# Six convolution units for eight in a spectral-mixing kernel, with transposes, late rows and one bank's products moved

## The chip, the cores and the metric

The kernel runs on one core of a Trainium2 chip. A core has five engines with queues of their own: TensorE (PE, with its weight loads as PEld), VectorE (DVE), ScalarE (ACT), GpSimd (POOL) and SyncE (SP). Here POOL issues all loads, which cast float32 in HBM to bfloat16 in the on-chip memory, and SP issues the stores. The metric is the device time of one execution in microseconds (us). The kernel before takes 172.97 us, the median of 3 runs (172.96 to 173.03).

## The reference, cut to what matters

`x` is [8, 3264, 192], `weight` [8, 7], `moe_w_r` and `moe_w_i` [64, 192, 192], `moe_w_ch` [192, 192], all float32.

```python
w = softmax(weight, axis=-1)                       # 8 heads of 24 channels, 7 taps
c[b, s, h, :] = sum_k w[h, k] * x_pad[b, s + k, h, :]   # causal: 6 zero rows ahead
X = rfft(c, axis=1)[:, :64]                        # 64 modes
Yr = Xr @ w_r - Xi @ w_i ; Yi = Xr @ w_i + Xi @ w_r     # per mode, 192 x 192
y = irfft(Y, n=3264)                               # all other modes are zero
u = c + y
out = u + max(u @ w_ch, 0)
```

## The kernel before, in words

**Layout.** The eight batches form four pairs q. A pair's 3264 rows are 13 blocks of 256 rows (the last holds 192), each of two tiles of up to 128 rows, and both batches of the pair stand side by side. `xall` holds all rows as bfloat16, one block per slot with a zero slot in front; the convolution reads it and overwrites it with `c`.

**Row stage.** `load_unit` (L147) issues the rows of a unit, a run of blocks of one pair, in two transfers (one per batch) and a third for the short last block. Units are 5 and 8 blocks for pair 0, then 7 and 6 for each other pair. `conv_step` (L306) convolves one of 8 heads and one of two row parities: four matmuls (L297) on 64-row quarters for the lower half, and, two steps later, four for the upper half; `turn` makes the two halves take a PSUM bank one after the other. ScalarE and VectorE evict the sums to `xall` (L334 to L344). Pair 0 uses double banks, the other pairs single ones. `dft` (L352) adds up the products of a pair's tiles with the table `ftab` of cosines and sines (L358), and `xtrans` (L366) turns the result to put channels on partitions, in `xt`. Pair 0's second transform and those of other units are called at a certain head of the next unit (`todo`, `dfts`). `idle` and the loop at L184 run matmuls that compute nothing.

**Mixing stage.** Sixteen groups of four modes; `mix` (L509) multiplies `xt` with a group's weights (L515), `mix_copy` (L520) scales the result into `ymix`, `mix_trans` (L542) transposes it into `yet`. The weights lie in 11 spots: five in `arena`, six in the last columns of `ct`. A group's weights are loaded by `load_w` (L272) into the spot that an earlier group has left. Between these, `some(n)` takes jobs from a list, `tjobs`: banks of eight transposes of `ftab` (`g_bank`), of products for `wsw` (`w_bank`), and of `c` (`c_bank`, L400, transposes at L398), whose results go to `ct`. One `c_bank` (columns 8 to 15) runs ahead, at the end of the row stage. `zw_pair` (L594) makes the products of `yet` with `wm` and `w1` for pairs 1 to 3 from all but the last eight modes; `late_rows` (L529) adds these modes' rows later by 16 transfers issued by POOL.

**Ring stage.** For every tile of the output, the products of `c` with the channel matrix, of the inverse table with the channel-multiplied spectrum ("g") are summed in a PSUM bank, `clamp` (L636) takes the maximum with zero, then the inverse table times the spectrum ("y") is added, and `add` (L611) adds `c` and issues the store. Duos 0 and 1 (a duo is a block's two tiles) are written out ahead; the 100 others go through a ring of eight PSUM banks, written as `lower` and `upper` halves of 64 rows (L716).

**Order.** All engines follow the order written in the program. POOL has eight completion semaphores for its loads; each load waits for the completion of the one eight before it. The order around mixing 15 before is: `zw_pair(3)`, `mix_trans`, mixing 15, then

```python
    place[1], ze = ze, sl[2:4]
    both(1, 0, "c", begin=True)
    mix_trans(d, 1, 1)
    both(1, 1, "c")
    for b in range(2):
        zw_mm(b, zm[b][:, 0:D], 0)
```

Of the kernel before, what the change touches and what calls it, by code (L numbers as in the profile page):

```python
# [20 lines left out]
def kernel(  # L21
# [26 lines left out]
    NIDLE = 85  # L48
    UNITS0 = ((0, 5), (5, 8))
    UNITS = ((0, 7), (7, 6))  # L50
    units = [(q, b0, n) for q in range(NQ) for b0, n in (UNITS if q else UNITS0)]

# [94 lines left out]
    def load_unit(q, b0, n):  # L147
        nf = min(n, NB - 1 - b0)
        s0 = NB * q + b0 + 1
        for i in range(2):  # L150
            off = ((2 * q + i) * S + 2 * P * b0) * D
            src = bass.AP(tensor=x.tensor, offset=x.offset + off, ap=[[2 * D, P], [2 * P * D, nf], [1, 2 * D]])
            nc.gpsimd.dma_start(out=xin[:, s0:s0 + nf, 2 * D * i:2 * D * (i + 1)], in_=src)  # L153
        if nf < n:
            off = (2 * q * S + 2 * P * (NB - 1)) * D
            src = bass.AP(tensor=x.tensor, offset=x.offset + off, ap=[[2 * D, PL], [S * D, 2], [1, 2 * D]])
            nc.gpsimd.dma_start(out=xin[0:PL, s0 + nf, :].rearrange("p (i c) -> p i c", i=2), in_=src)  # L157
# [106 lines left out]
    for k, u in enumerate(units[4:]):  # L264
        load_unit(*u)
        if k == 1:
            nc.gpsimd.dma_start(out=wm[:, 0:D], in_=moe_w_ch[0:P, :])
        if k == 2:
# [17 lines left out]
    def conv_pieces(step, row):  # L286

        (q, b0, n, h, a), z, _ = step
        s0 = NB * q + b0 + 1
# [14 lines left out]
    def conv_step(u):  # L304
# [3 lines left out]
        if u is not None:  # L308
            if u[0]:
                z = free.pop(0)  # L310
            else:
                z = flow[-2][0][2] if u[4] else free.pop(0)
            flow[-1] = [(u, z[:, u[4] if u[0] == 0 else 0, :], z), []]
# [11 lines left out]
        if old is None or old[0][0][4] == 0:  # L325
            return
        (q, b0, n, h, _), _, tile1 = old[0]
        s0 = NT * q + 2 * b0
        dst = xall[:, s0:s0 + 2 * n, :, GRP * h:GRP * h + GRP].rearrange("p (b a) i e -> p a b i e", a=2)
        tile0 = flow[-2 - CONVLAG][0][2]  # L330
        if q == 0:
            srcv = tile0[:, :, 0:2 * GRP * n].rearrange("p a (b i e) -> p a b i e", b=n, i=2)
            if h in ((0, 1, 2, 3, 4, 6) if b0 == 0 else (0, 1, 3, 5)):
# [18 lines left out]
    def dft(q, t0, t1):  # L352

        z = free.pop(0)
        xp = z[:, 0, 0:2 * D]
        for t in range(t0, t1):
            k = PL if t >= NT - 2 else P
            nc.tensor.matmul(xp, ftab[0:k, t, :], xall[0:k, NT * q + t, :, :],  # L358
                             start=(t == t0), stop=(t == t1 - 1), skip_group_check=True)
        if t0 == 0:  # L360
            nc.scalar.copy(out=xacc, in_=xp)
        else:
            nc.vector.tensor_tensor(out=xs[q % 2][:, :, :].rearrange("p i d -> p (i d)"), in0=xp, in1=xacc, op=ALU.add)
# [57 lines left out]
    for step in range(4):  # L421
        table(step, *PA)
    chores = {(0, 0): [(PB, (0,))], (0, 5): [(PA, (4,))], (0, H): [(PA, (5,)), (PB, (1, 2, 3)), (PC, range(4))],
              (1, H): [(PC, (4, 5))]}
# [12 lines left out]

    for k, u in enumerate(units):
        for h in range(H):
# [3 lines left out]
            if k > 1 and h == (4 if k == 2 else 2):  # L443
                if pend:
                    xtrans(pend.pop(0))
                dfts()
# [3 lines left out]
        if u[0]:  # L450
            todo.append((u[0], 2 * u[1], 2 * (u[1] + u[2])))
# [4 lines left out]
        if k == 0:  # L456
# [4 lines left out]
            idle(3)  # L461
        else:
# [3 lines left out]
            todo.append((0, PA[1], NT))  # L466
    flush()

    z = free.pop(0)
    c_bank(8, z[:, 0, :].bitcast(BF16))  # L470
    free.append(z)
# [30 lines left out]
    tjobs += [(c_bank, k) for k in range(0, 3 * NT * NQ, 8) if k != 8]  # L502

    def some(n):
        for _ in range(n):
            if tjobs:
# [3 lines left out]
    def mix(g, bank):  # L510
        yp = bank[:, D * (g % 2):D * (g % 2) + D]
        for j in range(3):
            for p4 in range(4):
# [3 lines left out]
                                 tile_position=(0, 32 * p4), skip_group_check=True)  # L517
        load_w(g + NW + NL)
# [10 lines left out]
    def late_rows(bank):  # L529

        m0 = MODES - 8
        for t in range(2):
            nc.tensor.matmul(bank[:, 0:2 * D], yet[:, t, 2 * B * m0:2 * B * MODES], (wm, w1)[t][:, :], start=(t == 0), stop=(t == 1),
                             skip_group_check=True)
        nc.scalar.copy(out=ylate, in_=bank[:, 0:2 * D])  # L535
# [6 lines left out]
    def mix_trans(d, g0, n):  # L542
        et = [z.bitcast(BF16)[:, 0:n * P].rearrange("p (g k) -> p g k", g=n) for z in ze]
# [50 lines left out]
    def zw_pair(q, bw, by):  # L594

        for t, bank in enumerate((bw, by)):
            for i in range(2):
                zw_mm(2 * q + i, bank[:, D * i:D * i + D], t)
        for t, bank in enumerate((bw, by)):
            dst, srcv = zwl[:, 2 * q - 2:2 * q, t, :], bank[:, 0:2 * D].rearrange("p (b d) -> p b d", b=2)  # L600
            if t == 0:
# [48 lines left out]
    some(2)  # L650
    xtrans(NQ - 1, ze)
    some(2)
    ND = NG // 2

    for d in range(ND - 2):
        mix(2 * d, zm[d % 2])
        mix(2 * d + 1, zm[d % 2])
        mix_copy(d, zm[d % 2], 0, 2)
        some(3)
        mix_trans(d, 0, 2)  # L660
        some(3)
    d = ND - 2
    mix(2 * d, zm[0])
    some(99)
    mix(2 * d + 1, zm[0])
    mix_copy(d, zm[0], 0, 2)
    sl = [z[:, 0, :] for z in open_psum("left", (1, 1, 1, 1))]
    place[0] = sl[0:2]
    both(0, 0, "c", begin=True)
    mix_trans(d, 0, 2)  # L670
    both(0, 1, "c")
    zw_pair(1, ze[0], ze[1])
    zw_pair(2, sl[2], sl[3])
    d = ND - 1
    mix(NG - 2, zm[1])
    mix_copy(d, zm[1], 0, 1)
    zw_pair(3, zm[0], sl[2])
    mix_trans(d, 0, 1)
    mix(NG - 1, zm[1])
    mix_copy(d, zm[1], 1, 1)  # L680

    place[1], ze = ze, sl[2:4]
    both(1, 0, "c", begin=True)
    mix_trans(d, 1, 1)
    both(1, 1, "c")
    for b in range(2):
        zw_mm(b, zm[b][:, 0:D], 0)
# [121 lines left out]
```

## Time and profile before

| What | Value |
|---|---|
| median of 3 runs | 172.97 us |
| profiled execution: time, span | 173.26 us, 171.5 us |
| TensorE busy, matmuls | 161.1 us (94%), 2897 |
| VectorE, ScalarE, POOL busy | 128.3, 113.7, 51.8 us |
| loads by POOL: bytes written, share of the DMA engines | 19.62 MB, 71.4% |
| stores by SP: bytes, share | 20.09 MB, 31.9% |
| convolution, L297 | 1024 matmuls, busy 38.6 us |
| transposes of c, L398 | 312 matmuls, busy 19.8 us |
| ring products, L716 | 34% of the chain that ended last |
| granted clock of TensorE | 0.997 |

The profile is one execution; its span runs from the first to the last instruction, and its time has 1.76 us around the span. Busy times of TensorE are modelled ends of pipelined matmuls. In a line of a group or a timeline, the operands stand as output<-input; "idle before" names what released an engine that had waited.

### The profile page before, as it was taken

The page shows a single profiled execution, that of the slowest core. Times are in us where ns is not written, and L with a number is a line of the kernel's source. Part 1 is how long each engine was busy: PE and PEld are TensorE (multiplying, and loading weights), DVE is VectorE, ACT ScalarE, POOL GpSimd, SP SyncE. Part 2 cuts the span into 40 slices and gives each one's busy share as a digit, 9 for nine tenths or more (in the row PEclk, how much of TensorE's full clock was granted, in tenths as well). Part 3 has the DMA queues.
Part 4 walks back from the last instruction along what each step waited for, and adds up shares of the span by engine and source line. Part 5 has one row for each costly group of instructions (what it writes and reads, how often), then busy time and mean ns, then how long its engine had stood idle before and what let it go on. Part 6 is the DMA issues. An engine that isn't in the chain of part 4 may idle for free.

```text
span 171.5 us, 6925 instructions
## 1 busy us (share of the span) xinstructions
PE 161.1 (94%) x2897; PEld 134.8 (79%) x2897; DVE 128.3 (75%) x262; ACT 113.7 (66%) x226; POOL 51.8 (30%) x93
## 2 busy tenths in 40 slices
PE   6998989999998999979999999999999999999980
PEld 6984867877867687669999875699898989898950
DVE  4899964637747384567776846799998999999990
ACT  8485874546546274277777664688888888888870
POOL 7998432424322453444432000790000000000000
PEclk9999999999999999999999999999999999999998
DMA  2999999999999999999999950489999989999995
GB/s 30 202 203 204 204 208 198 204 203 202 205 202 205 210 204 207 207 206 207 206 206 207 206 90 4 147 303 351 340 330 344 345 320 352 345 333 336 334 360 193
DMA packets 37151, 40.14 MB, mean 234 GB/s; under 512 B 2464, under 2 KB 37120, under 8 KB 37120
## 3 DMA queue, kind: packets, MB, share of 16 engines
q0 software_dynamic: 22816, 19.62, 71.4%
q1 hardware_dynamic: 14304, 20.09, 31.9%
q8 instruction: 22, 0.36, 0.8%
q14 instruction: 9, 0.07, 0.1%
HBM read 39.10 MB, written 20.05 MB: 345 GB/s over the span
## 4 chain that ended last, share of the span: by engine, by line
PE 80%; DMA 10%; POOL 3%; ACT 2%; issue 1%; DVE 0%; POOLq 0%; ACTq 0%; DVEq 0%
PE z L716 34%; PE z L297 16%; PE z L398 12%; DMA xall<-in_x_dram 10%; PE z L358 10%; PE z L515 3%; POOL xall L153 3%; PE z L647 1%; PE z L591 1%; PE z L375 1%; PE z L592 1%; PE z L582 1%; ACT ftab L393 1%; ACT z L479 1%; POOL xall L157 0%
## 5 line engine op out<-in xcount | busy, mean ns | idle before, releaser
L629 DVE TENSOR_TENSOR arena<-z,xall 128x384 f32<-128x384 f32 (+1 forms) x103 | 56.4, 557 | 3.4 <-PE z L716 1.5
L640 ACT ACTIVATE z<-z 128x384 f32<-128x384 f32 x102 | 48.5, 475 | 12.2 <-PE z L716 2.4
L716 PEld LDWEIGHTS <-ct 64*128 64x128 bf16 x600 | 42.3, 94 | 3.7 <-PE z L647 0.6
L716 PE MATMUL z<-arena,ftab 64*128 64x384 bf16 x308 | 44.9, 322 | 0.0
L297 PE MATMUL z<-xall,shared 64*64 64x336 bf16 (+3 forms) x1024 | 38.6, 294 | 1.8 <-DMA xall<-in_x_dram 1.0
L297 PEld LDWEIGHTS <-shared 64*64 64x64 bf16 x1024 | 33.2, 106 | 7.4 <-issue 4.9
L716 PE MATMUL z<-wsw,ct 64*128 64x192 bf16 x300 | 35.1, 243 | 0.0
L344 DVE CAST xall<-z 128x336 bf16<-128x336 f32 (+1 forms) x48 | 22.9, 483 | 12.5 <-PE z L297 10.2
L716 PEld LDWEIGHTS <-ftab 64*128 64x128 bf16 x396 | 29.7, 93 | 2.7 <-issue 0.5
L342 ACT CAST xall<-z 128x336 bf16<-128x336 f32 (+1 forms) x48 | 20.1, 418 | 15.4 <-PE z L297 11.3
L716 PE MATMUL z<-wm,ct 64*128 64x192 bf16 x200 | 29.9, 243 | 0.0
L716 PE MATMUL z<-w,ct 64*128 64x192 bf16 x100 | 24.3, 243 | 0.0
L395 DVE COPY ct<-z 128x1024 bf16<-128x1024 bf16 x27 | 17.4, 686 | 5.5 <-PE z L398 2.4
L398 PE MATMUL z<-ident,xall 128*128 128x128 bf16 x312 | 19.8, 219 | 0.0
L358 PE MATMUL z<-xall,ftab 128*128 128x384 bf16 (+1 forms) x104 | 18.3, 327 | 0.7 <-DVE xall L336 0.7
L398 PEld LDWEIGHTS <-xall 128*128 128x128 bf16 x312 | 17.8, 98 | 1.0 <-issue 0.2
L153 POOL DMA_DIRECT2D xall<-in_x_dram x16 | 14.7, 930 | 9.9 <-DMA xall<-in_x_dram 9.1
L358 PEld LDWEIGHTS <-ftab 128*128 128x128 bf16 (+1 forms) x104 | 9.6, 98 | 8.0 <-issue 1.2
L716 PE MATMUL z<-mixa,ftab 64*128 64x384 bf16 x88 | 13.6, 323 | 0.0
L393 ACT COPY ct<-z 128x1024 bf16<-128x1024 bf16 x12 | 12.1, 1012 | 2.1 <-PE z L398 1.9
L539 POOL DMA_DIRECT2D arena<-xs x16 | 7.9, 504 | 16.6 <-ACT xs L535 16.6
L184 PE MATMUL z<-xall 128*128 128x144 bf16 x85 | 7.9, 276 | 1.6 <-DVE xall L171 1.6
(113 smaller groups left out, 155.0 us busy)
## 6 DMA issues: line engine op xcount, KB each, us to landing
out_dram<-arena SPq DMA_DIRECT2D x47, 384.0 KB, 3.4
xall<-in_x_dram POOLq DMA_DIRECT2D x8, 672.0 KB, 16.8
xall<-in_x_dram POOLq DMA_DIRECT2D x8, 480.0 KB, 16.8
arena<-in_moe_w_r_dram POOLq DMA_DIRECT2D x10, 288.0 KB, 11.1
arena<-in_moe_w_i_dram POOLq DMA_DIRECT2D x10, 288.0 KB, 11.2
ct<-in_moe_w_r_dram POOLq DMA_DIRECT2D x6, 288.0 KB, 11.4
ct<-in_moe_w_i_dram POOLq DMA_DIRECT2D x6, 288.0 KB, 11.5
out_dram<-arena SPq DMA_DIRECT2D x4, 288.0 KB, 3.2
```

The source lines that it names most:

```text
L153: nc.gpsimd.dma_start(out=xin[:, s0:s0 + nf, 2 * D * i:2 * D * (i + 1)], in_=src)
L184: nc.tensor.matmul(free[3][:, 0, 0:144], zeros[:, 0:P], zeros[:, 0:144], start=True, stop=True, skip_group_check=True)
L297: yield nc.tensor.matmul(o, band[r, h, int(a != a1), c0:c0 + 64], xin5[r, s1:s1 + n, :, a1, dsl], start=(row == 0 and a1 == 0), stop=(row ...
L342: nc.scalar.copy(out=dst[:, a], in_=srcv)
L344: nc.vector.tensor_copy(out=dst[:, a], in_=srcv)
L358: nc.tensor.matmul(xp, ftab[0:k, t, :], xall[0:k, NT * q + t, :, :], start=(t == t0), stop=(t == t1 - 1), skip_group_check=True)
L393: nc.scalar.copy(out=out, in_=in_)
L395: nc.vector.tensor_copy(out=out, in_=in_)
L398: nc.tensor.matmul(o, in_, ident[:], start=True, stop=True, is_transpose=True)
L629: nc.vector.tensor_tensor(out=o[0:pn, :, a, :], in0=srcv, in1=xall[0:pn, s + a, :, :], op=ALU.add)
L640: nc.scalar.activation(out=z, in_=z, func=ACT.Relu)
L716: mm = nc.tensor.matmul(target(bank[k], cols, r), l, r, start=first, stop=last, skip_group_check=True)
```

## The change

Six units of 5, 8, 9, 10, 10 and 10 blocks run over the 52 blocks without regard to pairs; `parts_of` splits a unit at the border of pairs for its loads and its transforms. The first transfer of the first batch is split into two blocks and three. Seven idle matmuls are added at L184 and three are taken out after the first transform. Pair 0's second transform is called directly after its last unit; for its first ten tiles it takes the columns of six heads first and of two heads after. Of the banks of transposes of `c`, four run ahead of unit 3, two ahead of unit 4 and one after the last unit (`fill`). Half of one table step goes from the end of unit 1 to its sixth head. In the mixing stage `some` takes no bank whose place in `ct` still holds weights (`clear`). `zw_pair` makes products 384 columns wide, a batch to a bank. Bank 0 of the ring gets its `c` products before mixing 15; the last `mix_trans` and pair 0's y products use the bank `sl[2]`, pair 0's w products share `zm[0]`; the matmuls of the late rows come ahead of the g products, in `zm[1]`; the ring's banks have another order.

```diff
-    NIDLE = 85
-    UNITS0 = ((0, 5), (5, 8))
-    UNITS = ((0, 7), (7, 6))
-    units = [(q, b0, n) for q in range(NQ) for b0, n in (UNITS if q else UNITS0)]
+    NIDLE = 92
+    UNITS = (5, 8, 9, 10, 10, 10)
+    units = [(sum(UNITS[:k]), n) for k, n in enumerate(UNITS)]
...
+    def parts_of(g0, n):
+        while n > 0:
+            q, b0 = divmod(g0, NB)
+            m = min(n, NB - b0)
+            yield q, b0, m
+            g0, n = g0 + m, n - m
+
+    def load_unit(g0, n):
+        for part in parts_of(g0, n):
+            load_part(*part)
+
+    def load_part(q, b0, n):
         nf = min(n, NB - 1 - b0)
         s0 = NB * q + b0 + 1
-        for i in range(2):
...
+        pieces = [(0, 0, 2), (0, 2, nf - 2)] if q + b0 == 0 else [(0, 0, nf)]
+        for i, d, m in pieces + [(1, 0, nf)]:
...
-    def dft(q, t0, t1):
+    def dft(q, t0, t1, early=0):
...
+        DE = 6 * GRP
+        work = [(t, slice(0, DE)) for t in range(t0, t0 + early)] + [(t, slice(DE, D)) for t in range(t0, t0 + early)]
+        work += [(t, slice(0, D)) for t in range(t0 + early, t1)]
...
-              (1, H): [(PC, (4, 5))]}
+              (1, 5): [(PC, (4,))], (1, H): [(PC, (5,))]}
...
+    def fill(n):
+        for _ in range(n):
+            z = free.pop(0)
+            c_bank(8 * next(early_banks), z[:, 0, :].bitcast(BF16))
+            free.append(z)
+
+    early_banks = iter(range(1, 9))
     for k, u in enumerate(units):
+        fill({3: 4, 4: 2}.get(k, 0))
         for h in range(H):
             for a in range(2):
                 conv_step((*u, h, a))
             tables(k, h)
-            if k > 1 and h == (4 if k == 2 else 2):
-                if pend:
+            if k > 1 and h in (2, 6):
+                if pend and (k, h) != (2, 2):
                     xtrans(pend.pop(0))
-                dfts()
+                if h == 2:
+                    dfts()
...
-            idle(3)
         else:
...
-            todo.append((0, PA[1], NT))
+            dft(0, PA[1], NT, 10)
+            pend.append(0)
     flush()
-    z = free.pop(0)
-    c_bank(8, z[:, 0, :].bitcast(BF16))
-    free.append(z)
+    fill(1)
     dfts()
...
+    def clear(f, a):
+        last = a[0] + 7 - (3 * NT * NQ - NL * WGB // P) if f is c_bank else -1
+        return last < 0 or NW + last // (WGB // P) < mixed[0]
+
     def some(n):
         for _ in range(n):
-            if tjobs:
+            if tjobs and clear(tjobs[0][0], tjobs[0][1:]):
...
     def zw_pair(q, bw, by):
-        for t, bank in enumerate((bw, by)):
-            for i in range(2):
-                zw_mm(2 * q + i, bank[:, D * i:D * i + D], t)
...
+        for i, bank in enumerate((bw, by)):
+            b = 2 * q + i
+            last = 2 * MODES * B - B + b + 1
+            for t, w in enumerate((wm, w1)):
+                nc.tensor.matmul(bank[:, 0:2 * D], yet[:, t, b:last:B], w[:, :], start=(t == 0), stop=(t == 1),
+                                 skip_group_check=True)
...
+    def lower_c(k):
+        for j, p in enumerate(pieces(k, 0, "c")):
+            product(k, 0, p, j == 0, False)
+
     some(2)
     xtrans(NQ - 1, ze)
-    some(2)
+    some(4)
...
+    ring = [sl[3], zm[0], sl[2]] + sl[0:2] + ze + zm[1:2]
...
     mix_trans(d, 0, 1)
+    take(0)
+    lower_c(0)
     mix(NG - 1, zm[1])
     mix_copy(d, zm[1], 1, 1)
-    place[1], ze = ze, sl[2:4]
+    place[1] = ze
     both(1, 0, "c", begin=True)
-    mix_trans(d, 1, 1)
+    mix_trans(d, 1, 1, sl[2])
     both(1, 1, "c")
     for b in range(2):
-        zw_mm(b, zm[b][:, 0:D], 0)
+        zw_mm(b, zm[0][:, D * b:D * b + D], 0)
     for b in range(2):
-        zw_mm(b, ze[1][:, D * b:D * b + D], 1)
+        zw_mm(b, sl[2][:, D * b:D * b + D], 1)
+    late_mm(zm[1])
     nc.vector.tensor_copy(out=zw[:, 0, 0, :], in_=zm[0][:, 0:D])
-    nc.scalar.copy(out=zw[:, 0, 1, :], in_=zm[1][:, 0:D])
-    nc.vector.tensor_copy(out=zw[:, 1, 0:2, :].rearrange("p b d -> p (b d)"), in_=ze[1][:, 0:2 * D])
+    nc.scalar.copy(out=zw[:, 0, 1, :], in_=zm[0][:, D:2 * D])
+    nc.vector.tensor_copy(out=zw[:, 1, 0:2, :].rearrange("p b d -> p (b d)"), in_=sl[2][:, 0:2 * D])
...
-    ring = ze + zm[1:2] + place[0] + place[1] + zm[0:1]
...
     for k in range(LAG):
-        take(k)
-        for j, p in enumerate(pieces(k, 0, "c")):
-            product(k, 0, p, j == 0, False)
+        if k:
+            take(k)
+            lower_c(k)
         whole(k, "g")
         clamp(place[k][0], False)
         clamp(place[k][1])
-    late_rows(zm[0])
+    late_rows(zm[1])
```

## The prediction

> **What bounds the kernel now.** I read the slices of the page first, then TensorE's waits, then the moment at which the last weights arrive, then the POOL queue that issues the loads.
>
> The two rows of the page below (40 slices of 4.29 us) show two regimes: up to slice 22 (98.6 us) the DMA engines are full at a flat 202 to 210 GB/s, while TensorE is nearly full too; after slice 24 the outputs leave and TensorE is full alone.
>
> ```profile
> PE   6998989999998999979999999999999999999980
> DMA  2999999999999999999999950489999989999995
> GB/s 30 202 203 204 204 208 198 204 203 202 205 202 205 210 204 207 207 206 207 206 206 207 206 90 4 147 303 351 340 330 344 345 320 352 345 333 336 334 360 193
> ```
>
> TensorE's waits between 24 and 104 us (waiter, releaser, total us, times, longest): 3.1 us in 80. Only 0.7 us of it is for rows, at the start of pair 1; later no unit waits for its rows.
>
> ```profile
> PE z L515 <- ACT mixa L386: 1.0, 1, 1.0
> PE z L297 <- issue: 0.9, 1, 0.9
> PE z L297 <- DMA xall<-in_x_dram: 0.7, 1, 0.7
> PE z L582 <- DVE yet L552: 0.3, 1, 0.3
> PE z L398 <- ACT shared L527: 0.2, 1, 0.2
> ```
>
> The end of the load stream, by windows (length; busy us and instructions of PE, PEld, DVE, ACT, POOL; granted clock, DMA share, GB/s), and TensorE around mixing 15, the last matmuls that need a weight, by timeline:
>
> ```profile
> 95.00:100.00 5.00, 4.81 (x90) 3.85 (x88) 3.67 (x8) 3.05 (x5) 0.00 (x0) 1.00 1.16 199
> 100.00:101.00 1.00, 1.00 (x13) 1.00 (x14) 0.15 (x1) 0.48 (x1) 0.00 (x0) 1.00 0.56 92
> 101.00:102.00 1.00, 1.00 (x21) 0.75 (x19) 0.96 (x2) 0.63 (x2) 0.00 (x0) 1.00 0.26 44
> 102.00:104.00 2.00, 1.69 (x30) 1.21 (x28) 0.67 (x3) 1.20 (x4) 0.00 (x0) 1.00 0.00 0
> ```
>
> ```profile
> 102.66 0.46 PE L515 MATMUL z<-arena,mixa 128*16 128x192 bf16 x12
> 103.43 0.26 PE L582 MATMUL z<-wm,ct 64*128 64x192 bf16 x2 [0.31 <-DVE yet L552]
> 105.53 0.50 PE L647 MATMUL z<-mixa,ftab 128*128 128x384 bf16 x2
> 106.65 0.33 PE L533 MATMUL z<-wm,yet 128*128 128x384 bf16 x1
> 107.07 0.50 PE L716 MATMUL z<-mixa,ftab 64*128 64x384 bf16 x2
> ```
>
> The reader is to see that the stream dries up between 100 and 102 us (the trace records the last weight transfer's completion at 102.02) and that mixing 15 starts at 102.66, only 0.64 us later. Both TensorE and the stream are within a microsecond of being the bound; shortening TensorE's work ahead of mixing 15 pays at most until TensorE stands at 102.02. From 108.9 the ring runs 936 matmuls of line 716 in 56.8 us without a wait, and the change leaves these products alone: what mixing 15 and the steps up to the ring gain, the end gains.
>
> **The change, part by part.**
>
> Convolution in six units instead of eight. In the trace a head's 16 matmuls start every 0.44, 0.49, 0.57 and 0.65 us in units of 5, 6, 7 and 8 blocks: 0.081 us a block and next to nothing fixed. The 52 blocks cost the same 33.8 us; 256 fewer matmuls gain at most 0.01 us x 16 heads, taken as 0. Evictions: VectorE 458 ns (288 wide) and 508 (336) give about 658 at 480, under the 0.81 us that a head of ten blocks takes: hidden.
>
> Start. The first transfer has two blocks (256 rows) instead of five. The first issue took 1.02 us; POOL transfers of 192 and 256 rows took 0.61 to 0.71. The stream starts about 0.3 us earlier (ends: 0 and 0.4). A third issue now stands before the iota that the masks wait for, so the first conv moves from 9.47 to about 10.1 (seven more idle matmuls of 0.093 us end there); three idle matmuls of 0.8 us less before unit 1 pay for it, and unit 1 starts at about 17.5 (17.67).
>
> Pair 0's transform is no longer inside unit 2 but before it. Its evictions lag, so ten tiles first take the six heads that are ready. It fills the 0.92 us that TensorE stood from 23.45 to 24.36 for unit 2's rows; with the 0.15 above TensorE is 1.0 us ahead. The split adds ten short matmuls, 0.15 us.
>
> Six more banks of transposes before mixing (52 transposes take 3.01 us: 0.46 a bank, 2.8 us in all). They leave the mixing stage and enter the row stage; TensorE gains only where it would have stood. Do rows make it wait? Completions fit t = 4.9 us + MB/0.2 within 0.5 (9.34 at 0.98 MB, 24.34 at 3.88, 55.17 at 10.1). The new units' rows then land, less 0.3: unit 2 at 26.0, 3 at 35.6, 4 at 45.2, 5 at 55.0. TensorE arrives at 27.3, at 33.7 (four banks: 35.6), 45.6 (two: 46.5) and 57.1, from 0.081 us a block, 0.170 a transform tile (14 in 2.38), 0.2 per switch. Unit 3's rows just meet the banks; else they cover nothing. VectorE's copies (686 ns) lie beside. The last transform waits longer for the wider last eviction: 0.25 us.
>
> The hole of 1.0 us before mixing 0 now holds a transpose bank and the w products (0.65). The guard that keeps transposes off live weight spots moves two banks from the fifth pass to the sixth, both ahead of mixing 12: order only, 0.
>
> So TensorE, with pair 0's c products of the ring (0.35) put ahead, could start mixing 15 at 102.66 - 1.0 - 0.65 + 0.35 + 0.15 + 0.25 = 101.75 if a stall like the 0.9 us "issue" (in the middle of a unit, released by nothing shown) comes again, at 100.9 if not; ends 100.5 and 103.1. I take 101.3.
>
> The stream: 21 row transfers instead of 20, same bytes; POOL waits for a transfer's completion eight transfers back. Thirteen instead of ten stand before POOL's 5 us of memsets and selections, the thirteenth is released at about 17, the fourteenth issued near 22.6 (15.7 before), while bytes for 35.9 us are in flight: covered. The last weight lands at 102.02 - 0.3 = 101.7. Its sixteen parts completed from 99.64 to 102.02, elsewhere they spread 1.3, so ends 100.7 and, with one uncovered issue of 0.95, 103.0.
>
> Mixing 15 starts at the later of the two, about 101.85: 0.8 us gained.
>
> From mixing 15 to the ring (4.41 us before). Gone: the 0.31 wait on yet (mixing's transposes get a bank of their own, sl[2]) and 0.35 of c products. New: pair 0's w and y halves share a bank. Before, VectorE and ScalarE copied the w half in parallel out of two banks (104.86 for 0.36, 104.95 for 0.32). Now both columns lie in one bank, and in the program's order ScalarE's copy waits for VectorE's; VectorE starts after four products, not two. From the first zw product: 0.67 + 0.36 + 0.09 + 0.32 + 0.06 = 1.5 us to the first g product against 1.17 before; late_mm, 0.33, lies inside it. First zw product: 1.45 after mixing 15 instead of 1.70; g at 2.95; then 0.43 + 0.35 + 0.43 to the ring: 4.15. Gain 0.3; in parallel it would be 0.65, and if the copies wait for more, 0. By the Trainium skill, "PSUM — Partial Sum Buffer", section on PSUM bank collisions, any two engines on one bank and partition quadrant must be kept apart, two readers too; so the serial order is not one to be lifted, and by this rule the gain is 0.3, by the two parallel copies of the trace 0.65.
>
> The 16 late-row transfers follow a copy behind the same clamps; they land by 118.74 now, pair 1's products come near 121. Hidden, 2 us to spare. Pairs 1 to 3's zw products in half as many matmuls of double width: 8 x 0.083 against 4 x 0.163, nothing.
>
> Sum: -0.8 - 0.3 = -1.1 us. The profiled execution took 173.26 (span 171.5, 1.76 around it), 0.29 over the median; it would give 172.15, and the median 172.97 - 1.1 = **171.9**.
>
> **Rivals.**
>
> *More*: the stream's slowest engine spreads less and no fetch stall comes, mixing 15 starts at 101.0, copies nearly overlap: -1.65 - 0.3 = 171.0. For it: the spread of 1.3 seen before 65 us. Against: 2.3 to 2.7 in every transfer after.
>
> *The transposes fill nothing*: TensorE waited only 0.7 us for rows, so work moved forward is work all the same; it reaches mixing 15 at 102.6 and only the last 0.3 remains: 172.65. Against: the stood time above, and the hole before mixing 0.
>
> *Rows late (the other side)*: unit 3's rows come d later than 35.6. Each later unit costs TensorE 10.8 us and the stream 9.4, so the delay is carried to mixing 15 undiminished: 101.3 + d. It turns into a loss from d = 1.7. At d = 2.4 mixing 15 starts at 103.7: 173.7. For it: POOL's five waits of up to 3.0 us for row transfers, smaller transfers in its eight places, memsets between. Against: 13 us of bytes in flight at that point.
>
> *One transfer too many in a full stream*: its issue (0.67 to 0.95 us) is not covered, the last weight lands near 103.0, mixing 15 at 103.0: 173.0. Against: weight transfers of 288 KB flow at the same 203 to 207 GB/s as rows of 672 KB. The Trainium skill, "DMA: Bandwidth & Descriptors", on the anatomy of one software-issued DMA, gives each about 2.0 us fixed, and its Bandwidth section asks for 1 MiB per transfer. By that, an estimate, the last weight lands 2 us later and the time is 173.8; the flat GB/s row speaks against it.
>
> **How the numbers follow.** Forecast 0.50, more 0.17, nothing filled 0.13, rows late 0.15, one transfer too many 0.05. No change means within 0.35 us (0.2%), what a measurement of this kernel can tell. Faster: 0.50 + 0.17 + half of "nothing filled" = 0.74; same: the other half and one transfer too many, 0.11; slower: rows late, 0.15. The range leaves a tenth on each side: below, the 'more' case at its better half, 170.9; above, most of "rows late", 173.4.
>
> **What would show it.** Right: mixing 15 waits on a weight's DMA and starts between 101.5 and 102.2; the first g product waits for ScalarE's copy; ring 4.1 us after mixing 15; unit 3's first conv near 35.7. Wrong: mixing 15 after 102.7 with no DMA wait (TensorE late), a DMA row below 200 GB/s before 98 us, unit 3 or 4 waiting for rows over 1.5 us, or new waits in the ring.

## The result and the profile after

The changed kernel takes 175.23 us (median of 6 runs, 174.3 to 176.52), the kernel before in the same session 173.14 us (172.96 to 173.56). The ratio is 1.012, 95% interval 1.0075 to 1.017: slower by 2.1 us, where the forecast was 171.9 and its range ended at 173.4. The profiled execution took 174.3 us, span 172.2, so 2.1 us lie around the span where it was 1.76 before. It is the shortest of the six and shows 1.0 of the 2.1 us (174.3 against 173.26 in the profile of before); what the longer ones lost beyond that stands in no trace of this kernel.

The slices of the page of the changed kernel (4.30 us each):

```profile
DMA  2999999999999999999999970389989999999896
GB/s 39 145 193 204 204 204 203 203 204 203 202 204 204 206 207 206 207 206 206 209 203 206 208 121 5 104 293 335 367 318 342 348 325 349 338 345 337 322 360 228
```

Against the flat row of before, the second slice has 145 GB/s instead of 202 and the third 193. Everything after them is as full as it was, and the end has moved out: slice 23 carries 121 GB/s instead of 90. The first 11 us by windows, for the changed kernel (columns as in the windows of before: PE, PEld, DVE, ACT, POOL, clock, DMA share, GB/s):

```profile
3.00:4.00 1.00, 1.00 (x12) 1.00 (x9) 0.00 (x0) 0.98 (x2) 0.92 (x3) 1.00 0.66 95
4.00:5.00 1.00, 1.00 (x11) 1.00 (x10) 0.86 (x6) 0.58 (x1) 1.00 (x3) 1.00 1.05 136
5.00:6.00 1.00, 1.00 (x11) 1.00 (x9) 0.62 (x6) 0.62 (x2) 1.00 (x2) 1.00 1.15 166
6.00:7.00 1.00, 1.00 (x12) 1.00 (x9) 0.90 (x5) 0.99 (x2) 1.00 (x4) 1.00 1.15 144
7.00:8.00 1.00, 1.00 (x15) 1.00 (x14) 1.00 (x6) 0.13 (x1) 1.00 (x3) 1.00 1.14 127
8.00:9.00 1.00, 1.00 (x19) 1.00 (x17) 1.00 (x6) 0.72 (x2) 1.00 (x2) 1.00 1.11 161
9.00:10.00 1.00, 1.00 (x19) 1.00 (x17) 0.95 (x6) 0.96 (x3) 1.00 (x2) 1.00 1.22 173
10.00:11.00 1.00, 0.30 (x5) 0.11 (x2) 0.92 (x4) 0.02 (x1) 0.49 (x1) 1.00 1.32 202
```

The same windows of before read 62, 188, 202, 200, 204, 201, 204 and 205 GB/s. Two of them as they stand:

```profile
3.00:4.00 1.00, 1.00 (x12) 1.00 (x10) 0.51 (x1) 0.97 (x2) 0.95 (x3) 1.00 0.80 62
7.00:8.00 1.00, 1.00 (x20) 1.00 (x18) 1.00 (x6) 0.33 (x2) 1.00 (x2) 1.00 1.31 204
```

The stream does start earlier, 95 against 62, but then stays thin until POOL has ended its first run of issues at 10.5 us. From 3 to 11 us, 1204 KB pass instead of 1466: 262 KB or 1.3 us at 204 GB/s. Unit 0's rows are complete at 12.01 (9.34 before) and the last weight lands at 103.81 (102.02).

The trace records sixteen completions for each transfer, and these tell how the loss lasts. Those of the last transfer of unit 0 come from 8.83 to 9.34 before and from 9.01 to 12.01 after; those of the last weight from 99.64 to 102.02 before and from 100.16 to 103.81 after. The first part is 0.2 and 0.5 us later, the last part 2.7 and 1.8. So the lag made at the start is still there at 100 us, and a reader of a transfer waits for its last part.

Not all of the spread at the end comes from the start. In the kernel before it is 0.5 at 9 us and 2.4 at 102, and one step makes 1.4 of the growth, at the transfer that lands at 67.9. It lies 2.1 us behind the start of a packet of 16 KB on the page's queue "q8 instruction" (65.8, 0.95 long). The kernel without the cut has such a step of 1.3 at 80.9, 2.1 us behind a packet of 0.97. The trace does not name the engine of a packet; that this one held up one of the sixteen is argued from the times, and no run tests it.

TensorE's waits in the changed kernel (waiter, releaser, total, times, longest):

```profile
PE z L311 <- DMA xall<-in_x_dram: 2.0, 2, 1.9
PE z L545 <- DMA arena<-in_moe_w_i_dram: 0.8, 1, 0.8
PE z L687 <- ACT mixa L769: 0.2, 1, 0.2
```

The first is the wait for unit 0's rows before the first convolution (12.15 us). After it no unit waits for rows by more than 0.2 us; TensorE and the stream both run late. The second is mixing 15, the third the first g product. TensorE around them, by timeline, in the changed kernel:

```profile
102.74 0.33 PE L707 MATMUL z<-wsw,ct 64*128 64x192 bf16 x2
103.86 0.46 PE L545 MATMUL z<-arena,mixa 128*16 128x192 bf16 x12 [0.79 <-DMA arena<-in_moe_w_i_dram]
105.33 0.30 PE L628 MATMUL z<-wm,yet 128*128 128x192 bf16 x1
106.37 0.33 PE L564 MATMUL z<-w,yet 128*128 128x384 bf16 x1
...
106.91 0.48 PE L687 MATMUL z<-mixa,ftab 128*128 128x384 bf16 x2 [0.21 <-ACT mixa L769]
108.11 0.49 PE L707 MATMUL z<-mixa,ftab 64*128 64x384 bf16 x2
```

Mixing 15 starts 0.05 us after its weight, 1.2 us later than before. From there the first g product comes 3.05 us later (2.87 before) and the ring 4.25 (4.41). The ring's 936 matmuls take 56.8 us as they did. So in this execution the loss is made in the first ten microseconds and carried to the end by the stream. A punctual last weight would not have made a gain of it: TensorE's own work ahead of mixing 15 ends at 103.07, 0.4 later than mixing 15 began before.

### The profile page after: what moved, and what is told of

Its sections match the earlier page's. It is cut to its first block, busy times and chain, and to the rows that moved or that the text cites. A ratio compares the mean times of both kernels' runs of the same rounds, so it can differ in the third digit from the quotient of the medians.

```text
span 172.2 us, 6356 instructions
## 1 busy us (share of the span) xinstructions
PE 161.2 (94%) x2643; PEld 127.3 (74%) x2643; DVE 125.5 (73%) x246; ACT 110.2 (64%) x210; POOL 51.4 (30%) x94
## 4 chain that ended last, share of the span: by engine, by line
PE 58%; DMA 33%; POOL 3%; issue 2%; ACT 1%; DVE 0%; POOLq 0%; DVEq 0%; ACTq 0%
PE z L707 34%; DMA arena<-in_moe_w_i_dram 19%; PE z L311 14%; DMA xall<-in_x_dram 8%; DMA ct<-in_moe_w_i_dram 7%; PE z L372 6%; POOL xall L167 2%; PE z L413 2%; PE z L687 1%; ACT xall L353 0%; PE z L545 0%; ACT z L680 0%; ACT arena L667 0%; PE z L390 0%; POOL arena L290 0%
## 5 line engine op out<-in xcount | busy, mean ns | idle before, releaser
L669 DVE TENSOR_TENSOR arena<-z,xall 128x384 f32<-128x384 f32 (+1 forms) x103 | 57.0, 557 | 2.5 <-PE z L707 0.8
L311 PE MATMUL z<-xall,shared 64*64 64x480 bf16 (+3 forms) x768 | 38.6, 338 | 2.4 <-DMA xall<-in_x_dram 2.0
L311 PEld LDWEIGHTS <-shared 64*64 64x64 bf16 x768 | 25.1, 106 | 13.6 <-issue 4.0
L355 DVE CAST xall<-z 128x480 bf16<-128x480 f32 (+1 forms) x32 | 20.6, 645 | 12.7 <-PE z L311 11.8
L353 ACT CAST xall<-z 128x480 bf16<-128x480 f32 (+1 forms) x32 | 17.5, 548 | 14.8 <-PE z L311 14.8
L410 DVE COPY ct<-z 128x1024 bf16<-128x1024 bf16 x27 | 18.4, 686 | 5.2 <-PE z L413 3.6
L372 PE MATMUL z<-xall,ftab 128*128 128x384 bf16 (+3 forms) x114 | 18.0, 312 | 0.2 <-DVE xall L355 0.2
L372 PEld LDWEIGHTS <-ftab 128*128 128x128 bf16 (+1 forms) x114 | 10.2, 98 | 7.6 <-issue 1.5
L198 PE MATMUL z<-xall 128*128 128x144 bf16 x92 | 8.7, 279 | 1.6 <-DVE xall L185 1.6
```

The source lines that it names most:

```text
L198: nc.tensor.matmul(free[3][:, 0, 0:144], zeros[:, 0:P], zeros[:, 0:144], start=True, stop=True, skip_group_check=True)
L311: yield nc.tensor.matmul(o, band[r, h, int(a != a1), c0:c0 + 64], xin5[r, s1:s1 + n, :, a1, dsl], start=(row == 0 and a1 == 0), stop=(row ...
L353: nc.scalar.copy(out=dst[:, a], in_=srcv)
L355: nc.vector.tensor_copy(out=dst[:, a], in_=srcv)
L372: nc.tensor.matmul(xp[:, :, ds], ftab[0:k, t, :], xall[0:k, NT * q + t, :, ds], start=(j == 0), stop=(j == len(work) - 1), skip_group_chec ...
L410: nc.vector.tensor_copy(out=out, in_=in_)
```

## The experiments

Times are medians; each ratio is to the kernel before on the same chip, with its 95% interval. "Around" is the time less the span, a mean over the runs. Line numbers of the changed kernel are used.

**Undo the cut of the first transfer.**

```diff
-        pieces = [(0, 0, 2), (0, 2, nf - 2)] if q + b0 == 0 else [(0, 0, nf)]
+        pieces = [(0, 0, nf)]
```

> The changed kernel with pair 0's first transfer whole again (five blocks, no two and three); all else as changed. Theory 'split': the split of the first transfer thins the load stream between 3 and 10 us (127 to 175 GB/s in the changed kernel against 200 and more), and that alone puts the last weight at 103.8 us. Then here: 200 GB/s or more from 4.5 us on, unit 0's rows complete by 9.5 (12.0 changed, 9.3 before), the last weight near 102, mixing 15 at 102.0 to 102.4, the ring 4.25 us after it, the time 172.3 to 172.8, granted clock 0.997 in all runs. Rival 'larger or more transfers': the stream is thinned by the nine-block transfers and the new order of loads; then the thin stretch from 3 to 10 us stays, the last weight stays at 103 to 104 and the time at 174 to 176.

172.98 us (10 runs), ratio 0.9999 (0.9987 to 1.0012); spans 170.7 to 171.1, around 2.14. That is above the 172.3 to 172.8 of the first theory, and the granted clock was 0.987 to 1.000 instead of 0.997 throughout; its other numbers came, the rate within 3 GB/s. The windows of this kernel:

```profile
4.00:5.00 1.00, 1.00 (x11) 1.00 (x10) 0.97 (x6) 0.58 (x1) 1.00 (x2) 1.00 1.23 187
5.00:6.00 1.00, 1.00 (x11) 1.00 (x9) 0.63 (x4) 0.40 (x2) 1.00 (x3) 1.00 1.32 197
7.00:8.00 1.00, 1.00 (x19) 1.00 (x17) 1.00 (x6) 0.34 (x2) 1.00 (x2) 1.00 1.33 206
```

The stream is full again, the last weight lands at 102.10, mixing 15 starts at 102.14 and the ring 4.26 later. The cut is the whole loss; the rest of the change comes to nothing.

**The cut alone, in the kernel before.**

```diff
-        for i in range(2):
+        pieces = [(0, 0, 2), (0, 2, nf - 2)] if q + b0 == 0 else [(0, 0, nf)]
+        for i, d, m in pieces + [(1, 0, nf)]:
```

> The kernel before with the split of the first transfer and nothing else. Theory 'split': the stretch from 3 to 10 us falls to 130 to 175 GB/s, unit 0's rows are complete near 12 instead of 9.3, the last weight lands near 103.8 and mixing 15 starts near 103.9 instead of 102.66: 174.0 to 174.8, and more in runs in which TensorE's clock falls while it waits for unit 0. Rival 'larger or more transfers': 172.6 to 173.1, with over 200 GB/s from 4.5 us on.

174.47 us (6 runs), ratio 1.0086 (1.0059 to 1.0112). The windows of this kernel:

```profile
5.00:6.00 1.00, 1.00 (x18) 1.00 (x16) 0.62 (x6) 0.60 (x2) 1.00 (x2) 1.00 1.25 183
6.00:7.00 1.00, 1.00 (x20) 1.00 (x18) 0.90 (x5) 0.99 (x2) 1.00 (x4) 1.00 1.07 121
7.00:8.00 1.00, 1.00 (x20) 1.00 (x18) 1.00 (x6) 0.15 (x1) 1.00 (x3) 1.00 1.19 154
```

Last weight 103.74, mixing 15 at 103.79. The cut does the same harm with eight units and the old tail, so it needs none of the other parts.

**The tail alone** (the ring's first bank ahead, the new banks, the shared bank of the w half, `zw_pair` 384 wide, the late rows' matmuls ahead), behind the row stage of before. Three places of the edit are shown.

```diff
     mix_trans(d, 0, 1)
+    take(0)
+    lower_c(0)
     mix(NG - 1, zm[1])
...
-    mix_trans(d, 1, 1)
+    mix_trans(d, 1, 1, sl[2])
...
-    nc.scalar.copy(out=zw[:, 0, 1, :], in_=zm[1][:, 0:D])
+    nc.scalar.copy(out=zw[:, 0, 1, :], in_=zm[0][:, D:2 * D])
```

> The kernel before with the part from the end of mixing on as changed (products of zw 384 wide, ring bank 0's c ahead of mixing 15, pair 0's w half in one bank, late rows ahead of g), its row stage as before. From the changed kernel's trace, mixing 15 to the ring is 4.25 us there against 4.41: with mixing 15 up to 0.35 later where TensorE and not the weight is late, the time is 172.8 to 173.3, no change within 0.2%. If the serial copies cost nothing here, 172.4; if ScalarE's wait grows in this order, 173.5.

173.14 us (10 runs), ratio 1.0017 (0.9996 to 1.0037). Mixing 15 starts at 102.56, 0.6 after its weight (101.97); g comes 3.05 later and the ring 4.25 later. Here TensorE is the later of the two. The c products ahead of mixing 15 (0.35 in the forecast) would then use up the 0.16 saved behind it. That is argued, not shown: the time is unchanged, but in the profiled execution mixing 15 starts no later than the 102.66 of before.

**More idle matmuls.**

```diff
-    NIDLE = 92
+    NIDLE = 120
```

> The changed kernel with 120 idle matmuls instead of 92, so that TensorE is busy until about 12.9 us. Theory 'cold clock': the changed kernel's spread (174.3 to 176.5) comes from runs in which TensorE stands some 1.9 us for unit 0's rows and is granted a lower clock after it (0.977 to 0.987 over the span); then here every run has 0.997 and the times lie within 0.4 us, near 174.3 to 174.8. Rival 'stream': the spread comes from the load stream itself; then times spread by 1 us or more at a clock of 0.997.

175.84 us (4 runs, 174.62 to 176.73), ratio 1.0135 (1.0086 to 1.0183), at a granted clock of 0.992 to 0.995. With the clock up, the loss stays, the times still lie 2.1 us apart, and the thin stream stays too (126 and 129 GB/s at 6 to 8 us): the clock alone makes neither the loss nor the spread. A part of the spread may still go with it: of the changed kernel's six executions the two at 0.997 took 174.3 and 174.72 us, the four at 0.977 to 0.987 took 174.83 to 176.52. What TensorE's standing costs is not told here, since it still stands 0.96 us for unit 0's rows. In this profiled execution, of 176.73 us, it also waits 0.96 us for unit 1's rows and 1.26 for unit 3's, and the last weight lands at 104.81.

**The same cut in the second batch's transfer.**

```diff
-        pieces = [(0, 0, 2), (0, 2, nf - 2)] if q + b0 == 0 else [(0, 0, nf)]
-        for i, d, m in pieces + [(1, 0, nf)]:
+        pieces = [(1, 0, 2), (1, 2, nf - 2)] if q + b0 == 0 else [(1, 0, nf)]
+        for i, d, m in [(0, 0, nf)] + pieces:
```

> The changed kernel, but the first transfer keeps its five blocks and the second batch's transfer is the one cut into two and three blocks: as many transfers, the same bytes, only the short one is not the first. If it is the short first transfer that thins the stream (the engines begin with little work in flight), the stream runs at 200 GB/s or more from the fourth microsecond, unit 0's rows are there by about 9.6, the last weight lands at about 102.1, and the time is 173.0, as in the kernel without a cut. If any additional small transfer among the first ones does it (one more issue on POOL while nothing else is in flight), the rate stays below 180 GB/s up to about 10 us, the last weight lands near 103.7 and the time is 174.7 or more.

173.04 us (10 runs), ratio 1.0002 (0.999 to 1.0015): no loss, with as many transfers and the same bytes. In its profiled execution, of 173.56 us, the stream carries 161 to 191 GB/s up to 8 us, 202 after, and the last weight lands at 102.76; in between the two expectations on that point, with the first one on the time.

**The first transfer in four blocks and one.**

```diff
-        pieces = [(0, 0, 2), (0, 2, nf - 2)] if q + b0 == 0 else [(0, 0, nf)]
+        pieces = [(0, 0, 4), (0, 4, nf - 4)] if q + b0 == 0 else [(0, 0, nf)]
```

> The changed kernel with its first transfer cut into four blocks and one instead of two and three. If the harm comes from how little the first transfer holds (two blocks are 0.39 MB, four 0.79, five 0.98), most of it is gone: 180 GB/s or more from the fourth microsecond, last weight at 102.1 to 102.5, time 173.0 to 173.3. If it comes from a short transfer issued second, while the first runs, the rate stays under 180 GB/s until 9 us and the time is 174.5 or more.

174.47 us (4 runs), ratio 1.01 (1.0065 to 1.0135). The windows of this kernel:

```profile
5.00:6.00 1.00, 1.00 (x11) 1.00 (x9) 0.62 (x4) 0.81 (x2) 1.00 (x2) 1.00 1.31 201
6.00:7.00 1.00, 1.00 (x12) 1.00 (x10) 0.93 (x5) 0.93 (x2) 1.00 (x4) 1.00 1.25 179
7.00:8.00 1.00, 1.00 (x19) 1.00 (x17) 1.00 (x6) 0.00 (x0) 1.00 (x2) 1.00 1.18 184
8.00:9.00 1.00, 1.00 (x19) 1.00 (x17) 1.00 (x6) 0.89 (x3) 1.00 (x2) 1.00 1.20 180
```

Here the stream reaches 201 GB/s and falls back to 180. Last weight 104.23. From 3 to 11 us it carries 1328 KB, 128 less than the kernel without the cut (1456), where two and three blocks lose 252. So the rate at the start is nearer to the first expectation, the last weight and the time are nearer to the second's. How little the first transfer holds bears on the rate, but it is not the whole reason: with four blocks the time is lost all the same.

**Two blocks, then the whole second batch, then three.**

```diff
-        for i, d, m in pieces + [(1, 0, nf)]:
+        pieces.insert(1, (1, 0, nf))
+        for i, d, m in pieces:
```

> The changed kernel with the cut, but the order of the first three transfers is two blocks of the first batch, the five of the second batch, then the first batch's other three. If a short first transfer is enough, the stream is thin up to about 10 us as in the changed kernel, the last weight lands at 103.5 or later and the time is 174.5 to 175.2. If it takes two short ones in a row ahead of a long one, the long second transfer fills the engines: last weight near 102.2, time 173.0 to 173.3.

174.62 us (4 runs), ratio 1.0101 (1.0074 to 1.0129); 121, 149, 178, 143 and 155 GB/s from 4 to 9 us, last weight 103.41. A long second transfer does not mend it.

**The second batch whole first, then the first batch in two and three.**

```diff
-        for i, d, m in pieces + [(1, 0, nf)]:
+        for i, d, m in [(1, 0, nf)] + pieces if q + b0 == 0 else pieces + [(1, 0, nf)]:
```

> The changed kernel with the cut, but the second batch's whole transfer of five blocks is issued first and the first batch's two and three blocks after it. If what matters is that the very first transfer on the queue is a whole one, this is like the kernel with the cut in the second batch: 190 GB/s or more from the fifth microsecond, last weight at 102.1 to 102.8, time 173.0 to 173.2. If it is that the first batch's rows are fetched in two parts, wherever they stand, the stream is thin up to about 10 us and the time is 174.4 or more.

173.08 us (10 runs), ratio 1.0005 (0.9993 to 1.0018). The windows of this kernel:

```profile
4.00:5.00 1.00, 1.00 (x11) 1.00 (x10) 0.87 (x1) 0.58 (x1) 1.00 (x3) 1.00 1.18 172
5.00:6.00 1.00, 1.00 (x11) 1.00 (x9) 0.91 (x7) 0.00 (x0) 1.00 (x2) 1.00 1.32 204
6.00:7.00 1.00, 1.00 (x14) 1.00 (x12) 0.65 (x3) 0.73 (x2) 1.00 (x4) 1.00 1.30 197
7.00:8.00 1.00, 1.00 (x20) 1.00 (x18) 0.90 (x5) 0.99 (x2) 1.00 (x3) 1.00 1.29 195
```

Last weight 102.66. The very same two and three blocks of the first batch cost no time behind a whole transfer. What counts between these kernels is that the rows' first transfer on the queue is a whole one.

**A small load of another tensor first** (98 KB, rows whole).

```diff
+    nc.gpsimd.dma_start(out=wm[:, 0:D], in_=moe_w_ch[0:P, :])
     load_unit(*units[0])
...
-        if k == 0:
-            nc.gpsimd.dma_start(out=wm[:, 0:D], in_=moe_w_ch[0:P, :])
```

> The changed kernel without the cut, but with another small load, the channel matrix's first 128 rows (98 KB, issued behind the rows otherwise), as the very first on the queue. If any short transfer at the head of the queue thins the stream, it stays under 185 GB/s up to about 10 us, the last weight lands at 103.5 or later and the time is 174.4 or more. If it takes rows cut into parts, the whole transfers behind it fill the engines, all that is lost is one issue of 0.6 to 0.7 us: last weight 102.4 to 102.8, time 173.2 to 173.6.

173.96 us (4 runs), ratio 1.006 (1.0043 to 1.0078), above both of the second theory's numbers and under the first's. Last weight 103.09, 1.0 later than without the load. The stream is thin only up to 5 us (60 GB/s from 3 to 4 us, then this window) and near full from there (187 to 207):

```profile
4.00:5.00 1.00, 1.00 (x11) 1.00 (x10) 0.93 (x2) 0.58 (x1) 1.00 (x3) 1.00 0.92 103
```

By the completions, the thin start makes only a part of the 1.0. The middle of the sixteen of the last weight is 0.3 later (100.87 against 100.56); their spread is 3.2 instead of 2.3, after steps of 0.8 at 30.6 and 1.4 at 93.7, 2.6 and 2.0 us behind the start of a packet of instructions. So this kernel does not tell what a short transfer at the head costs by itself. It does tell that the long thin stretch came only where the rows at the head were cut.

**Without the last weight group, in the kernel before.**

```diff
-        load_w(g + NW + NL)
+        if g + NW + NL != MODES // 4 - 1:
+            load_w(g + NW + NL)
```

> The kernel before without the load of the last weight group (mixing 15 multiplies with what group 4 has left in that spot; the result of the last four modes is not the reference's). It shows when TensorE itself would be ready for mixing 15. If the kernel before usually waits for its last weight (the profile used for the forecast, with mixing 15 at 102.66 and 0.64 after the weight, being later than usual), mixing 15 starts 0.2 to 0.5 us earlier than usual, at 101.8 to 102.0, and the time is 172.4 to 172.7. If TensorE and not the weight holds it, as the profile of before has it, nothing is gained: 172.9, mixing 15 at 102.2 to 102.6.

173.18 us (10 runs), ratio 1.0009 (0.9994 to 1.0023), mixing 15 at 102.50 straight behind the matmuls ahead of it. The kernel before does not wait for its last weight; my suspicion that the profile used for the forecast was an unusual one falls.

**The same, in the changed kernel without the cut.**

> The changed kernel without the cut of the first transfer and without the load of the last weight group (mixing 15 multiplies with what group 4 has left there). If the row stage of the change does put TensorE ahead and only the stream holds mixing 15 back (it waited 0.70 us there in the kernel without the cut), mixing 15 starts at 101.3 to 101.5 and the time falls by 0.6 to 0.7, to 172.3. If TensorE's lead comes from nothing but the wait (other waits appear in its place, ymix, yet or the clock), mixing 15 stays at 101.8 to 102.1 and the time at 172.8 to 173.0.

172.21 us (6 runs), ratio 0.9954 (0.9935 to 0.9974), 0.77 under the kernel that only lacks the cut. Its median span is 0.55 shorter, 170.25; the rest lies around it (1.99 against 2.14). The time is the first expectation's; mixing 15 starts at 101.87, in the range of the second, but 0.6 earlier than in the kernel before without its last group (102.50). The timeline of this kernel, from an execution of 172.37 us:

```profile
101.62 0.33 PE L708 MATMUL z<-wsw,ct 64*128 64x192 bf16 x2
101.87 0.46 PE L545 MATMUL z<-arena,mixa 128*16 128x192 bf16 x12
103.34 0.30 PE L629 MATMUL z<-wm,yet 128*128 128x192 bf16 x1
```

Mixing 15 follows without a wait. TensorE's lead from the new row stage is real; in the whole kernel it stands and waits for the stream.

**Eight units, without the cut.**

```diff
-    UNITS = (5, 8, 9, 10, 10, 10)
+    UNITS = (5, 8, 7, 6, 7, 6, 7, 6)
```

> The changed kernel without the cut of the first transfer, with the eight units of before (5, 8, 7, 6, 7, 6, 7 and 6 blocks); all else of the change stays, the early transposes included. If the six units are worth nothing in themselves, as forecast (0.081 us a block, 256 matmuls more for the same blocks), TensorE is ready for mixing 15 where it was without the cut, 101.3 to 101.6, mixing 15 waits for its weight at 102.1 and the time is 172.9 to 173.1. If the fewer units are what put TensorE ahead (fewer switches, fewer short evictions), it is ready at 102 or later and the time is 173.2 to 173.6. The time around the span was 1.77 us with the row stage of before and 2.0 to 2.15 with the new one: if it goes with the number of units and their matmuls, it is 1.8 here; if with anything else of the row stage, 2.1.

172.86 us (10 runs), ratio 0.9996 (0.9982 to 1.001). TensorE is done with what stands ahead of mixing 15 at 101.5 (101.7 with six units), and waits for the weight (102.24). The spans are 0.2 longer in the mean, 171.06 against 170.84, and the time around them 0.37 shorter, 1.77 against 2.14.

**One copy for the w half, without the cut.**

```diff
-    nc.vector.tensor_copy(out=zw[:, 0, 0, :], in_=zm[0][:, 0:D])
-    nc.scalar.copy(out=zw[:, 0, 1, :], in_=zm[0][:, D:2 * D])
+    nc.scalar.copy(out=zw[:, 0, 0:2, :].rearrange("p b d -> p (b d)"), in_=zm[0][:, 0:2 * D])
```

> The changed kernel without the cut of the first transfer, and pair 0's w half leaves its bank in one copy of 384 columns on ScalarE instead of VectorE's and then ScalarE's of 192. If the serial copies are what makes the first g product late (3.05 us after mixing 15 instead of 2.95 or less), it comes after about 0.48 to 0.50 us of copy instead of 0.37 + 0.05 + 0.33: g at 2.8, the ring at 4.0 after mixing 15, and the time is 0.2 to 0.3 below the kernel without the cut: 172.7 to 172.8. If late_mm, the y products or another thing are in the way, g stays at 3.05 and the time at 173.0.

172.40 us (13 runs), ratio 0.9971 (0.996 to 0.9982): faster than both kernels. The median span is 0.3 shorter than without this edit (170.5 against 170.8); the other part of the gain lies around the span (1.98 against 2.14). Its profiled execution, of 174.43 us, can't show the step: from 104.0 to 107.4, between mixing 15 and the ring, TensorE's granted clock is 0.50 there. The step is read in the last experiment.

**Eight units and one copy, without the cut.**

> The changed kernel without the cut, with the eight units of before and with pair 0's w half leaving its bank in one copy on ScalarE: the parts of the change that the runs leave standing. If the two gains add (0.35 us outside the span with eight units, 0.3 us from the one copy), the time outside the span is 1.8, the span 170.8 and the time 172.5 to 172.6. If the time outside the span does not go with the units, or eight units let TensorE reach the ring later, it is 172.8 to 172.9.

172.61 us (12 runs), ratio 0.9981 (0.9969 to 0.9993); mean span 170.78, around 1.78. The timeline of this kernel:

```profile
102.17 0.47 PE L545 MATMUL z<-arena,mixa 128*16 128x192 bf16 x12 [0.82 <-DMA arena<-in_moe_w_i_dram]
104.39 0.48 ACT L768 CAST mixa<-z 128x384 bf16<-128x384 f32 x1 [0.56 <-PE z L629]
104.92 0.48 PE L687 MATMUL z<-mixa,ftab 128*128 128x384 bf16 x2
106.12 0.49 PE L707 MATMUL z<-mixa,ftab 64*128 64x384 bf16 x2
```

The copy of 0.48 us ends at 104.87 and g starts without a wait, 2.75 after mixing 15 instead of 3.05; the ring 3.95 after it instead of 4.25. It gains 0.25 over eight units with two copies, as expected; that eight units add to it is not borne out (172.61 against 172.40, with intervals that overlap).

## Why the prediction was wrong

**The step that failed** is the term for the cut: "the stream starts about 0.3 us earlier (ends: 0 and 0.4)", carried on as 102.02 - 0.3 = 101.7 for the last weight. I had priced the small first transfer by POOL's issue times alone, with no loss at either end. The start was indeed earlier (first issue 0.86 us instead of 1.02, 95 GB/s against 62 at 3 to 4 us). But then the engines carried 127 to 173 GB/s up to 10 us while transfers stood issued: at 4 us all 0.98 MB of unit 0 (as written) had been issued and 0.10 had passed. The last weight landed at 103.81, 1.8 later than before instead of 0.3 earlier, and beyond my own upper end of 103.0; with the cut undone it landed at 102.10. That the cut could change the rate behind it had no place in my sum, although no row of before showed a start with a short transfer. A bound on the side of a loss was wanted there. "Covered", the step beside it, held for what it was about: past 11 us the one more transfer and the later issues left the stream at 202 to 209 GB/s.

The sign I had named for being wrong, a DMA row below 200 GB/s before 98 us, is what came: 145 and 193. Of the rivals, "rows late" came nearest for mixing 15 (103.7 against 103.86), and the estimate from the Trainium skill's figure, under "one transfer too many", nearest in the time (173.8). The 2.0 us that the Trainium skill ("DMA: Bandwidth & Descriptors", anatomy of one software-issued DMA) gives as fixed per transfer came near the 1.8 us by which the last weight was later. But not by that mechanism: the kernel with the cut in the second batch has as many transfers and loses nothing. My argument against the rival, weights of 288 KB at full rate, was sound for the full stream and said nothing of its start.

**Rows late**: not in the profiled execution. Behind the first unit TensorE waited for rows no more than 0.2 us at a time; the delay came by the last weight, at the end of the same stream. In the longer execution with 120 idle matmuls unit 3 did wait for its rows, 1.26 us, behind the same thin start.

**The start.** First convolution forecast at 10.1, unit 1 at 17.5: 12.15, for want of rows, and 19.67. Without the cut 9.79 and 18.56, so unit 1 is late there too: TensorE stands 1.6 us before it, put down to "issue", and why is open.

**TensorE at mixing 15**, forecast 101.3. Without the cut its work ends at 101.7, 1.0 before the 102.66 of before instead of 1.4, well within the ends of 100.5 and 103.1. But the way there was not the forecast one: unit 3's first convolution, named as a sign at 35.7, came at 37.2 (38.3 with the cut). So 1.1 us of the lag were made up behind it by nothing that I had counted, and that only 0.4 is left at the end is in part luck. What each of the moves gave of this was not measured apart, but for the units: six are worth nothing there, as forecast.

**The last weight** without the cut is at 102.1, not 101.7: the 0.3 us was the cut's. So mixing 15 gains 0.52 (102.66 to 102.14) instead of 0.8.

**The ring.** Forecast 4.15 after mixing 15 with the copies one after the other, g at 2.95: 4.25 and 3.05 (4.41 and 2.87 before). The serial order was read rightly: VectorE's copy at 106.15 for 0.36, ScalarE's at 106.54 for 0.32, g at 106.91. The gain is 0.16 instead of 0.3, by 0.1 us more from mixing 15 to g. With one copy it is 0.46. The rule of the Trainium skill that I weighed there ("PSUM — Partial Sum Buffer", PSUM bank collisions: two engines on one bank are kept apart) named the right case, the serial one, and the trace agrees.

**What is left without the cut.** 0.52 + 0.16 = 0.68 off a span of 171.5 gives 170.8, which is the span measured. But the mean span of before is 171.1 to 171.2, so 0.3 of this is the distance of one profiled execution from the mean; I took 0.29 off for the median and kept the whole gain. The other 0.37 is lost around the span, 2.14 instead of 1.77, so the time is that of before. No row of a trace shows this time; it goes with the six units (in the mean 1.76 to 1.80 in all kernels with eight, 1.98 to 2.17 in all with six), and why is open.

**What stays open** is by what the cut thins the stream. Packets of 768 bytes take 0.079 us in the middle in every kernel; in the thin stretch up to 16 of them in a microsecond take more than 0.12, the longest 1.7, and the engines also stand about a seventh of the time. In the changed kernel it ends with POOL's run of issues, at 10.5 us. That would fit descriptors being written while they are read, but two runs speak against it as the whole reason: before, the same run of issues lies beside a full stream, and with four blocks and one the run ends at 10.3 while the stream is still at 184 and 191 GB/s from 12 to 14 us. The Trainium skill ("DMA: Bandwidth & Descriptors", SWDGE vs HWDGE vs iDMA) says that GpSimd writes the descriptors of such transfers into rings in SBUF. No run here shows the rings, and none explains why a whole first transfer protects those behind it.

## What to carry to other kernels

Where a queue has to be full from its first microsecond to its last, look at the DMA rate per microsecond of the first ten before touching the head of the queue; leave the first transfer whole and cut, if at all, behind it. A lead of one engine pays only up to the next resource: here TensorE gained a microsecond and the stream let half of it through. And set one profiled execution against the mean span of many before counting tenths.

## What the runs showed of the hardware

- A transfer of five blocks at the head of POOL's queue, cut in 2 + 3 or 4 + 1, puts the last weight 1.3 to 2.7 us later, a hundred microseconds on (103.41 to 104.81 against 102.10); behind a whole transfer the same cut costs 0.7 at most in the profiled executions, and nothing measurable in the time.
- What a part of the stream loses in the first 10 us it does not make up in the next 90, although the stream is full: against the kernel without the cut, the middle of the sixteen completions is 1.4 us later at the end of unit 0 and 1.3 at the last weight. The sixteen come 3.0 us apart at 12 us, 3.0 at 31 and 3.7 at 103 in the changed kernel; without the cut 0.7, 1.4 and 2.3.
- One ScalarE copy of 384 columns (0.48 us) is shorter than two of 192 on two engines out of one bank, one after the other (0.36, 0.03 between, 0.32).
